# Sixteen tiles transposed by DMA instead of TensorE, and a check and last sums moved earlier in an attention kernel

## The chip, the cores and the metric

The kernel runs on one core of a Trainium2 chip. The metric is the time of one execution on the device in microseconds. Before the change three runs took 743.94, 744.22 and 745.38 us; their median is 744.22 us.

## What is computed

Two blocks on separate inputs of shape (1, 2048, 640), in bf16, 32 heads of 20 columns each; the results stand side by side in an output of (1, 2048, 1280).

```python
# A: softmax attention
scores = jnp.einsum("bhqd,bhkd->bhqk", q, k) * (Dh ** -0.5)
p = _softmax(scores, axis=-1)
o = jnp.einsum("bhqk,bhkd->bhqd", p, v)          # then o @ wo
# B: linear attention
phi = lambda t: jnp.where(t > 0, t + 1, jnp.exp(t)) + 1e-6
kv = jnp.einsum("bhsd,bhse->bhde", pk, v)        # pk = phi(k), pq = phi(q)
num = jnp.einsum("bhqd,bhde->bhqe", pq, kv)
den = jnp.einsum("bhqd,bhd->bhq", pq, z)[..., None] + 1e-6
o = num / den                                     # then o @ wo
```

## The kernel before

The program is one straight list of instructions per engine. Class `_Fast` writes these lists when the kernel is built: `run` steps through a clock of its own, and at each step gives each engine the next operation that its own estimates call ready. The estimates are constants in the code (`_c_dve`, `_c_act`, `_c_pool`, and a number handed to `push` for each operation, `occ` for how long the engine is held and `lat` for when the result is seen). On the chip the lists are fixed and each engine works its list in order; semaphores guard what is read and written. An operation that is late therefore holds up everything behind it on its engine.

**A** is done in 32 rounds `n` (`self.NN`), one for each of 4 query chunks of 512 and 8 groups of 4 heads. A round has 16 key tiles `kt` of 128 keys. TensorE makes the scores of a key tile for four heads into PSUM; then there are two ways to their exponentials. On the common one, ScalarE reads two heads' scores (128x1024) in one ACTIVATE (L1854) and writes `f_PT`; one pass of value matmuls follows. For `DN[n]` of the 16 key tiles of round `n`, VectorE instead makes 16-bit integers from the scores (L1752, four instructions to a key tile, tile `f_Sr`), whose bits, read as bf16, stand for the exponential; GpSimd adds a constant to them twice (L1928), and TensorE takes them through three passes of value matmuls. `DN` sums to 139 of the 512 key tiles of all rounds.

The value matmuls of a round add up in one PSUM bank. `norm` (L1931) then has VectorE transpose that bank into `f_T` (L1958), take the reciprocal of the sums into `f_Rt` (L1949), have the product made (L1951, on GpSimd, in the last round on VectorE) and transposed again into `f_OTn` (L1955). DMAs on SP's queue move the rows to `f_OTd` (L1984), from where the output projection reads them as weights. In the last query chunk that projection comes in two parts: `step_open` makes the sums over all but the last group of heads, 8 of them (4 row tiles, 2 halves), each held in a PSUM bank; `step_close` adds the last group, VectorE (L989) and ScalarE (L988) copy the bank to `f_st`, and SP writes it out (L985).

**The check.** The short way to the exponential holds only for a range of sums. `check` (L2010) has GpSimd compare the reciprocals `f_Rt` with two bounds (L2018, L2020) and VectorE reduce the result (L2022); at the very end `step_flag` folds this to one number, `f_flag`, which all engines load (L2275); were it 0, a general version would run in its place. In the kernel before, the check over rounds 0 to 30 (496 columns) is queued in `normed` when round 30 is finished, and that over round 31 (16 columns) when round 31 is.

**B** is a list of steps (`self.qb`, made by `b_steps`) that TensorE works on where A leaves it time. Each step has a `pace`, the share of A's scores that must be behind it, rising from `B0` to `B1`. For each row tile `t` of the 16: `ndstep` makes numerator and denominator, VectorE divides into `self.o` (L1587, two buffers in `f_ar`); `trstep` transposes the 128x640 result with five TensorE transposes (L1004) into a PSUM bank, and VectorE copies them to `self.oT` (L1610); `ostep` multiplies by B's `wo`, twice 20 matmuls of 32x320, and the result is copied (L989) and written out (L985). `pick_step` picks TensorE's next step from the head of these lists. Before the change it posted a step without matmuls (a load) only when it stood first in `self.qb`.

SP's queue carries nearly all DMAs, in order: the pieces of Q and K that A's later rounds wait for (L1194), the `f_OTd` moves, B's input, which comes from DRAM through DMA transposes of 512x128 (L1362), and the outputs.

Of the kernel before, what the change touches and what calls it, by code (L numbers as in the profile page):

```python
# [7 lines left out]
BF16 = mybir.dt.bfloat16  # L8
# [6 lines left out]
D_MODEL = 640  # L15
# [3 lines left out]
N_DC = 5  # L19
# [749 lines left out]
class _Fast:  # L769
# [10 lines left out]
    WP = 0.7578125  # L780
    FADJ = False
    NX = 1
    DN = (4, 4, 4, 5, 4, 4, 4, 4, 5, 4, 5, 4, 5, 4, 4, 5, 4, 4, 5, 4, 5, 4, 5, 4, 5, 4, 5, 4, 4, 5, 4, 4)
    XD = 2
    HOT = 0
    PVH2 = 11
    B0 = 0.33
    B1 = 0.92
    LASTD = 8
    STEP = 20.0  # L790
    DMIN = -3
# [6 lines left out]
    def __init__(self, nc, sch, es, ps, A_x, A_wqkv, A_wo, B_x, B_wqkv, B_wo, out):  # L798
# [52 lines left out]
        self.pieces = {}  # L851
        self.abank = list(self.AUX)
        self.srr = 0
        self.stq = [[] for _ in range(4)]
        self.sth = {}
        self.log = []
# [534 lines left out]
    def b_steps(self):  # L1391
        ps = self.ps
        sch = self.sch
        NQC = self.NQC
        out = []
# [165 lines left out]
        def ndstep(tc, tl, h):  # L1561
            cs = (0, 1, 2) if h == 0 else (2, 3, 4)
            t = 4 * tc + tl
            key = ("nd", t, h)
            k = t % 2
# [24 lines left out]
            needs = tuple(("bq", tc, c) for c in cs)  # L1590
            p = before(t, 2)
            if p is not None:
                needs += (("tr", p),)
            return _Step(mms, post, needs=needs, key=key)

        def trstep(t):
            k = t % 2
            key = ("tr", t)

            def mms(b):  # L1600
                pb = ps[:, b, :].bitcast(BF16)
                for c in range(N_DC):
                    yield ("F", [dict(tr=True, out=pb[:, 128 * c:128 * (c + 1)], id=self.ident[:],
                                      reads=(("o", k, 0), ("o", k, 1), "ident"), writes=(("ps", b),),
                                      inc=(c == N_DC - 1), **{"in": self.o[:, k, 128 * c:128 * (c + 1)]})], 58.0)

            def post(b):
                pb = ps[:, b, :].bitcast(BF16)
                dst = self.oT[:, k].rearrange("p c m -> p (c m)")
                self.push("dve", lambda e: e.tensor_copy(dst, pb[:, 0:D_MODEL]), (("ps", b),), (("oT", k),),  # L1610
                          400, after=lambda: (self.done.add(key), self.abank.append(b)))
            needs = (("nd", t, 0), ("nd", t, 1))
            p = before(t, 2)
            if p is not None:
                needs += (("bo", p, 0), ("bo", p, 1))
            return _Step(mms, post, needs=needs, key=key)

        def ostep(t, h):
            k = t % 2
            key = ("bo", t, h)  # L1620

            def mms(b):
                for c in range(N_DC):
                    yield ("C", self.quad(b, 0, 320, self.oT[:, k, c, :], self.wB[:, c, D_MODEL + 320 * h:D_MODEL + 320 * (h + 1)],
                                          c == 0, c == N_DC - 1, (("oT", k), ("wB", 1))), 137.0)

            def post(b):
                if ("bs", t) not in self.pieces:
                    self.pieces["bs", t] = self.slot(("b", t))
                self.evac(b, self.pieces["bs", t], ("b", t), h, "dve", 2,  # L1630
                          self.out[128 * t:128 * (t + 1), D_MODEL:2 * D_MODEL], lambda: self.done.add(key))
            return _Step(mms, post, needs=(("tr", t), ("wl", 1, 1)), key=key)

        order_tc = list(range(NQC - 1, -1, -1))
        prev = ("turn", "ld2")
# [325 lines left out]
    def normed(self, n):  # L1961
# [35 lines left out]
                    self.prio.append(self.step_out(t, h, range(5), needs=tuple(  # L1997
                        ("OTs", self.pos[qc, x]) for x in range(N_GRP)), cb=odone))
        if g == N_GRP - 2 and last:
            self.sch.barrier(("dve", "pool"), tuple(x for k in range(self.NQC) for x in self.xt(k)))  # L2000
            for t in range(4 * qc, 4 * qc + 4):
                for h in range(2):
                    self.prio.append(self.step_open(t, h, tuple(("OTs", self.pos[qc, x]) for x in range(6)) + ("expd", "dd")))
            self.check(0, n)
        if g == N_GRP - 1 and last:
            for t in range(4 * qc, 4 * qc + 4):
                for h in range(2):
                    self.prio.append(self.step_close(t, h))
            self.check(n, n)

    def check(self, n0, n1):
        k = 0 if n0 == 0 else 1
# [43 lines left out]
        return self.NN  # L2056

    def pick_step(self, t):
        while self.qb and self.qb[0].mms is None and self.runnable(self.qb[0]):
            st = self.qb.pop(0)  # L2060
            st.post(None)
            self.done.add(st.key)
        for k, st in enumerate(self.prio):
            if st.bank is not None and self.runnable(st):
                gen = st.mms(self.obank[st.bank])
                it = next(gen)
                if self.est("pe", [r for m in it[1] for r in m["reads"]], ()) > t + 30:
                    continue
                self.prio.pop(k)
                return [st, self.obank[st.bank], gen, it]  # L2070
# [11 lines left out]
        for q in cands:  # L2082
# [4 lines left out]
            for k in ks:  # L2087
                st = q[k]
                if st.mms is None:
                    break  # L2090
# [255 lines left out]
```

## Time and profile before

| | |
|---|---|
| median of 3 runs | 744.22 us (743.94 to 745.38) |
| the profiled execution's own time | 744.1 us |
| its span, first to last instruction | 742.3 us |
| instructions | 25718 |
| busy: TensorE, ScalarE, GpSimd, VectorE | 721.4, 711.3, 595.6, 591.1 us |
| ScalarE's ACTIVATE of L1854 | 746, together 698.2 us |
| granted TensorE clock, mean | 0.998 |

The busy time of an engine counts each moment once, also where one instruction starts before the one ahead of it has ended, as ScalarE's and TensorE's do. So the mean of one ACTIVATE (1139 ns) is longer than the step from one to the next. What 1.8 us separate the execution's own time from its span lies outside the instructions.

### The profile page before, as it was taken

The numbers are of one execution on the slowest core, as the hardware profiler recorded it, in microseconds if no ns is written. First come the engines' busy times: TensorE is split into PE (matmuls) and PEld (weight loads), VectorE is DVE, ScalarE is ACT, GpSimd is POOL, SyncE is SP. The second block draws the span as 40 slices with busy tenths as digits, with TensorE's granted clock in tenths as the row PEclk, the third lists the DMA queues.
The fourth block names the chain that finished last, engine by engine and source line by source line (L and its number), as shares of the span: only waits on it lengthen the run. The fifth ranks groups of instructions, "written<-read, shape, count | busy, mean of one in ns | idle before, by whom it ended". The sixth has DMA issues, their size and how long they took to land.

```text
span 742.3 us, 25718 instructions
## 1 busy us (share of the span) xinstructions
PE 721.4 (97%) x11214; PEld 256.0 (34%) x11214; DVE 591.1 (80%) x1136; ACT 711.3 (96%) x806; POOL 595.6 (80%) x359
## 2 busy tenths in 40 slices
PE   8999999999899999999999999999999999999996
PEld 5433333332223333333333333233233333332334
DVE  6888887958747788787879878799898878898962
ACT  4879999999999999999999999999999999999993
POOL 6687798779998787878778779886889778779774
PEclk9999999999999999999999999999999999999999
DMA  8520101007200100201001003011010100000001
GB/s 197 155 48 16 32 14 35 13 21 149 45 10 18 39 9 15 37 6 41 17 11 33 23 7 95 13 42 36 17 42 33 32 30 16 12 31 15 15 28 42
DMA packets 42610, 27.67 MB, mean 37 GB/s; under 512 B 26890, under 2 KB 41930, under 8 KB 42490
## 3 DMA queue, kind: packets, MB, share of 16 engines
q1 hardware_dynamic: 41178, 25.62, 13.5%
q8 instruction: 90, 1.47, 0.8%
q10 hardware_dynamic: 1312, 0.33, 0.2%
q14 instruction: 30, 0.25, 0.1%
HBM read 8.40 MB, written 5.24 MB: 18 GB/s over the span
## 4 chain that ended last, share of the span: by engine, by line
ACT 69%; PE 21%; POOL 4%; DVE 2%; DMA 1%; SPq 1%; issue 0%; ACTq 0%; DVEq 0%
ACT f_PT L1854 67%; PE ps L155 21%; ACT ps L1385 3%; POOL f_Sr L1928 3%; DMA f_ar<-in_A_wqkv_dram 1%; DVE f_Sr L1752 1%; SPq L1194 1%; DMA f_KT<-f_ar 0%; DVE f_ar L1234 0%; POOL f_ar L1419 0%; POOL f_ar L1416 0%; DVE f_KT L1255 0%; POOL f_xT L2020 0%; POOL f_xT L2018 0%; POOL f_ar L1422 0%
## 5 line engine op out<-in xcount | busy, mean ns | idle before, releaser
L1854 ACT ACTIVATE f_PT<-ps 128x1024 bf16<-128x1024 f32 x746 | 698.2, 1139 | 15.2 <-PE ps L155 14.5
L1928 POOL TENSOR_SCALAR f_Sr<-f_Sr 128x2048 int16<-128x2048 int16 x278 | 527.4, 1897 | 87.5 <-PE ps L155 67.1
L1752 DVE TENSOR_SCALAR f_Sr<-ps 128x512 int16<-128x512 f32 x556 | 376.0, 684 | 73.4 <-PE ps L155 65.8
L155 PE MATMUL ps<-f_Qr,f_KT 32*128 32x512 bf16 x2048 | 293.4, 384 | 7.3 <-ACT f_PT L1854 5.0
L155 PEld LDWEIGHTS ps<-f_Qr,f_KT 32*128 32x128 bf16 x2048 | 74.0, 91 | 250.1 <-ACT f_PT L1854 233.4
L155 PE MATMUL ps<-f_ar 128*32 128x320 bf16 (+4 forms) x3024 | 152.1, 295 | 1.5 <-DVE f_Sr L1752 0.7
L155 PE MATMUL ps<-f_PT,f_V 128*21 128x512 bf16 x1492 | 141.7, 383 | 0.0
L155 PE MATMUL ps<-f_Sr,f_V 128*21 128x512 bf16 x1112 | 100.9, 382 | 2.1 <-POOL f_Sr L1928 1.9
L155 PEld LDWEIGHTS ps<-f_ar 128*32 128x32 bf16 x3024 | 61.1, 95 | 65.3 <-issue 35.2
L1951 POOL TENSOR_TENSOR f_T<-f_T,f_Rt 128x512 bf16<-128x512 f32 x31 | 32.5, 1048 | 41.5 <-DVE f_Rt L1949 40.0
L155 PE MATMUL ps<-f_Sr,f_Vp 128*21 128x512 bf16 x556 | 54.8, 382 | 0.2 <-POOL f_Sr L1928 0.2
L155 PEld LDWEIGHTS ps<-f_PT,f_V 128*21 128x21 bf16 x1492 | 35.7, 90 | 47.0 <-issue 40.9
L1387 DVE SCALAR_TENSOR_TENSOR f_ar<-ps,f_ar 128x320 bf16<-128x320 f32 (+1 forms) x52 | 29.2, 561 | 13.7 <-ACT ps L1385 13.0
L155 PE MATMUL ps<-f_ar,f_xT 128*32 128x160 bf16 x1280 | 37.1, 234 | 1.3 <-DMA f_ar<-in_A_wqkv_dram 0.7
L155 PEld LDWEIGHTS ps<-f_Sr,f_V 128*21 128x21 bf16 x1112 | 25.4, 90 | 34.1 <-issue 23.0
L989 DVE CAST f_st<-ps 128x320 bf16<-128x320 f32 x60 | 28.5, 479 | 10.1 <-PE ps L155 10.1
L1383 DVE TENSOR_SCALAR f_ar<-ps 128x320 f32<-128x320 f32 (+1 forms) x52 | 29.0, 558 | 7.7 <-PE ps L155 7.5
L1385 ACT ACTIVATE ps<-ps 128x320 f32<-128x320 f32 (+1 forms) x52 | 33.4, 643 | 0.0
L155 PE MATMUL ps<-f_wo,f_OTd 128*32 128x320 bf16 (+1 forms) x608 | 32.7, 302 | 0.0
L155 PE MATMUL ps<-f_xT,f_ar 128*32 128x512 bf16 x400 | 30.3, 383 | 0.3 <-DVE f_xT L1168 0.2
L155 PEld LDWEIGHTS ps<-f_ar,f_xT 128*32 128x32 bf16 x1280 | 24.0, 96 | 17.6 <-issue 8.9
L155 PE MATMUL ps<-f_xT,f_wq 128*32 128x512 bf16 x320 | 25.2, 383 | 0.0
(76 smaller groups left out, 325.1 us busy)
## 6 DMA issues: line engine op xcount, KB each, us to landing
out_dram<-f_st SPq DMA_DIRECT2D x32, 160.0 KB
f_ar<-in_B_wqkv_dram SPq DMA_DIRECT2D x3, 800.0 KB
f_OTd<-f_OTn SPq DMA_DIRECT2D x105, 20.0 KB
f_Qr<-f_sq SPq DMA_DIRECT2D x88, 20.0 KB
f_KT<-f_ar SPq DMA_DIRECT2D x22, 80.0 KB
f_ar<-in_A_wqkv_dram SPq DMA_DIRECT2D x2, 800.0 KB
f_wq<-in_A_wqkv_dram SPq DMA_DIRECT2D x1, 800.0 KB
f_wo<-in_A_wo_dram SPq DMA_DIRECT2D x1, 800.0 KB
```

Source lines behind the costliest of these rows:

```text
L155: lambda e: e.matmul(out, lhsT, rhs, start=start, stop=stop, tile_position=tp, skip_group_check=sgc),
L989: (lambda e: e.tensor_copy(sl, ps[:, b, 0:320])), (("ps", b),), (("stage", s, h),),
L1194: self.push("sp", lambda e, d=d, a=a, m=m: e.dma_start(d, src[a:a + m, :]), rs, res, 710, prio=n if which == "Q" else g, after=after, ok=okd)
L1383: self.push("dve", lambda e: e.tensor_scalar(r1, src, 0.0, 1e-6, op0=ALU.max, op1=ALU.add), (("ps", b),), (rk,), _c_dve(n), prio=1, ok=ok, ...
L1385: "act", lambda e: e.activation(src, src, AF.Exp), (), (("ps", b),), _c_act(n), prio=0,
L1387: "dve", lambda e: e.scalar_tensor_tensor(dst, src, 1.0, r1, op0=ALU.min, op1=ALU.add),
L1752: post = lambda: self.push("dve", lambda e: e.tensor_scalar(self.Sr[:, s, i, :], self.ps[:, b, :], 0.0, 32639.0 - self.PH[-1], op0=ALU.max ...
L1854: return _Op("act", lambda e: e.activation(self.PT[:, s0:s0 + n, :], ps[:, b0:b0 + n, :], AF.Exp, scale=math.log(2.0) / 128.0, bias=self.l ...
L1928: return e.tensor_scalar(v, v, inc, 1.0, op0=ALU.add, op1=ALU.mult)
L1951: nmul, lambda e: e.tensor_tensor(T2v, Tv, R.unsqueeze(2).broadcast_to([128, 16, 32]), op=ALU.mult),
```

## The change

The change has four parts.

1. `trstep` has no matmuls any more. Its `issue` puts five DMA transposes of 128x128 on SP's queue, from `self.o` to `self.oT`, both in on-chip memory (L1603 of the changed kernel); the code gives each 1300 ns of SP's time and 3500 ns to its landing. `ostep` waits for each of the five pieces by itself. 80 TensorE transposes and 16 VectorE copies go, 80 DMA transposes come.
2. `check` over the first rounds is queued as soon as the last Q is made and A has no preparing steps left; it then covers the rounds that are finished (0 to 27, 448 columns), and the last check covers rounds 28 to 31 (64 columns).
3. Three of the eight `step_open` no longer wait for the last ACTIVATE (`expd`) but for the last VectorE key tile (`dd`) and for B's list to be empty (`bfin`).
4. `DN` is 1 smaller in rounds 27 and 29, so it sums to 137, and `B1` is 0.93. `pick_step` posts a load or a transposing step wherever it stands in the first eight of B's list.

```diff
-    DN = (..., 5, 4, 4, 5, 4, 4)
+    DN = (..., 5, 3, 4, 4, 4, 4)
-    B1 = 0.92
+    B1 = 0.93
...
-            def mms(b):
-                pb = ps[:, b, :].bitcast(BF16)
+            def issue(b):
                 for c in range(N_DC):
-                    yield ("F", [dict(tr=True, out=pb[:, 128 * c:128 * (c + 1)], id=self.ident[:],
...
-                self.push("dve", lambda e: e.tensor_copy(dst, pb[:, 0:D_MODEL]), (("ps", b),), (("oT", k),),
-                          400, after=lambda: (self.done.add(key), self.abank.append(b)))
+                    self.push("sp", lambda e, c=c: e.dma_start_transpose(
+                        self.oT[:, k, c, :], self.o[:, k, 128 * c:128 * (c + 1)]),
+                        (("o", k, 0), ("o", k, 1)), (("oT", k, c),), 1300, prio=40, lat=3500,
+                        after=(lambda: self.done.add(("trd", t))) if c == N_DC - 1 else None)
...
         if g == N_GRP - 2 and last:
-            self.sch.barrier(("dve", "pool"), tuple(x for k in range(self.NQC) for x in self.xt(k)))
             for t in range(4 * qc, 4 * qc + 4):
                 for h in range(2):
-                    self.prio.append(self.step_open(t, h, tuple(("OTs", self.pos[qc, x]) for x in range(6)) + ("expd", "dd")))
-            self.check(0, n)
+                    self.prio.append(self.step_open(t, h, tuple(("OTs", self.pos[qc, x]) for x in range(6)) + (
+                        ("dd", "bfin") if 2 * (t % 4) + h < 3 else ("expd", "dd"))))
...
+        if last and self.chk < 0 and ("Q", self.NN - 1) in self.done and not self.qa:
+            self.sch.barrier(("dve", "pool"), tuple(x for k in range(self.NQC) for x in self.xt(k)))
+            self.chk = n
+            self.check(0, n)
...
-        while self.qb and self.qb[0].mms is None and self.runnable(self.qb[0]):
-            st = self.qb.pop(0)
+        for st in [x for x in self.qb[:8] if x.mms is None and self.runnable(x)]:
+            self.qb.remove(st)
```

What this does to the lists shows at three places. The first is VectorE's list at its end. Before, the reduction of the check (L2022) stands ahead of the last round's transpose (L1958):

```order
L989 CAST f_st<-ps 128x320 x2
L2022 TENSOR_REDUCE f_gm<-f_xT 128x1
L1958 STREAM_TRANSPOSE f_T<-ps 128x512
L1949 RECIPROCAL f_Rt<-f_T 128x16
L1951 TENSOR_TENSOR f_T<-f_T,f_Rt 128x512
L1955 STREAM_TRANSPOSE f_OTn<-f_T 128x512
```

The same place in the changed list (its line numbers differ a little: L1953 is L1958 of before, L1944, L1946 and L1950 are L1949, L1951 and L1955, L2021 is L2022):

```order
L990 CAST f_st<-ps 128x320 x2
L1953 STREAM_TRANSPOSE f_T<-ps 128x512
L1944 RECIPROCAL f_Rt<-f_T 128x16
L1946 TENSOR_TENSOR f_T<-f_T,f_Rt 128x512
L1950 STREAM_TRANSPOSE f_OTn<-f_T 128x512
L2021 TENSOR_REDUCE f_gm<-f_xT 128x1
```

The first reduction has left this place; the one of the last check stands behind the norm, as before.

The second is GpSimd's list where the first check now stands, three norms (L1946) from the end:

```order
L1923 TENSOR_SCALAR f_Sr<-f_Sr 128x2048 x7
L2017 TENSOR_SCALAR f_xT<-f_Rt 128x448
L2019 TENSOR_SCALAR f_xT<-f_Rt 128x448
L1946 TENSOR_TENSOR f_T<-f_T,f_Rt 128x512
L1923 TENSOR_SCALAR f_Sr<-f_Sr 128x2048 x9
```

and VectorE's list beside it:

```order
L1953 STREAM_TRANSPOSE f_T<-ps 128x512
L1388 SCALAR_TENSOR_TENSOR f_ar<-ps,f_ar 128x512
L1944 RECIPROCAL f_Rt<-f_T 128x16
L990 CAST f_st<-ps 128x320
L2021 TENSOR_REDUCE f_gm<-f_xT 128x1
L1747 TENSOR_SCALAR f_Sr<-ps 128x512 x2
L1950 STREAM_TRANSPOSE f_OTn<-f_T 128x512
```

The two comparisons and the reduction now stand between the work of a running round, ahead of GpSimd's product and of two of VectorE's score conversions.

The third is SP's list where B's first result tiles (L1603) come in, between B's input, the `f_OTd` moves and the pieces of Q:

```order
L1363 DMA_TRANSPOSE f_ar<-in_B_x_dram 128x512 x3
L1603 DMA_TRANSPOSE f_ar<-f_ar 128x128 x9
L1979 DMA f_OTd<-f_OTn 20x512 x3
L1979 DMA f_OTd<-f_OTn 4x512
L1979 DMA f_OTd<-f_OTn 16x512
L1603 DMA_TRANSPOSE f_ar<-f_ar 128x128 x5
L1195 DMA f_Qr<-f_sq 12x512
```

Before, the five loads of L1362 stood there in one piece, and the moves and the pieces of Q followed without anything between them.

## Rows read from the trace of the kernel before

**Rows 1.** The page's first part: busy time, share of the span and instructions.

```profile
PE 721.4 (97%) x11214; PEld 256.0 (34%) x11214; DVE 591.1 (80%) x1136; ACT 711.3 (96%) x806; POOL 595.6 (80%) x359
```

**Rows 2.** Busy time of each engine by stretch, granted clock, DMA share.

```profile
core 0: us, PE busy (x) PEld busy (x) DVE busy (x) ACT busy (x) POOL busy (x), PEclk, DMA share, GB/s
226.00:300.00 74.00, 73.01 (x1146) 25.63 (x1146) 58.88 (x108) 73.92 (x86) 61.59 (x35) 1.00 0.08 24
300.00:400.00 100.00, 99.69 (x1590) 34.85 (x1594) 81.22 (x151) 100.00 (x120) 77.61 (x43) 1.00 0.10 22
...
600.00:690.00 90.00, 88.12 (x1249) 28.55 (x1250) 75.03 (x145) 89.95 (x104) 72.85 (x41) 1.00 0.06 19
690.00:710.00 20.00, 19.64 (x325) 7.70 (x317) 18.42 (x47) 19.98 (x23) 15.76 (x9) 1.00 0.06 21
710.00:729.00 19.00, 18.22 (x257) 6.50 (x259) 7.25 (x14) 18.99 (x21) 17.49 (x10) 1.00 0.06 21
```

**Rows 3.** The chain that ended last, by time: start us, us, what.

```profile
546.56 69.72 ACT f_PT L1854 x76
...
629.11 46.76 ACT f_PT L1854 x51
```

**Rows 4.** Timeline of the end: start us, us, engine, line, operation, [idle before <-releaser].

```profile
714.13 14.86 ACT L1854 ACTIVATE f_PT<-ps 128x1024 bf16<-128x1024 f32 x16
...
715.72 22.47 SPq L985 DMA_DIRECT2D out_dram<-f_st  x6
...
729.34 0.48 PE L155 MATMUL ps<-f_PT,f_V 128*21 128x512 bf16 x4
...
729.56 0.82 PE L155 MATMUL ps<-f_wo,f_OTd 128*32 128x320 bf16 x16
...
730.24 0.82 PE L155 MATMUL ps<-f_wo,f_OTd 128*32 128x320 bf16 x16
...
730.76 1.19 DVE L2022 TENSOR_REDUCE f_gm<-f_xT 128x1 f32<-128x992 f32 x1 [9.29 <-POOL f_xT L2020]
...
731.86 0.71 DVE L1958 STREAM_TRANSPOSE f_T<-ps 128x512 f32<-128x512 f32 x1
...
734.39 1.13 PE L155 MATMUL ps<-f_wo,f_OTn 128*32 128x320 bf16 x28 [1.12 <-DVE f_OTn L1955]
734.83 1.68 DVE L989 CAST f_st<-ps 128x320 bf16<-128x320 f32 x4 [0.43 <-PE ps L155]
...
736.45 0.42 ACT L988 CAST f_st<-ps 128x320 bf16<-128x320 f32 x1 [0.41 <-PE ps L155]
736.62 0.14 DVE L2036 TENSOR_SCALAR f_flag<-f_g 1x1 int32<-1x1 f32 x1
```

**Rows 5.** Groups of instructions by line: busy us, mean ns, idle before, releasers.

```profile
L1928 POOL TENSOR_SCALAR f_Sr<-f_Sr 128x2048 int16<-128x2048 int16 x278 | 527.4, 1897 | 87.5 <-PE ps L155 67.1
L1752 DVE TENSOR_SCALAR f_Sr<-ps 128x512 int16<-128x512 f32 x556 | 376.0, 684 | 73.4 <-PE ps L155 65.8 <-DMA f_KT<-f_ar 0.7
L1004 PE MATMUL ps<-f_id,f_ar 128*128 128x128 bf16 x100 | 10.1, 222 | 0.0
L1610 DVE COPY f_ar<-ps 128x640 bf16<-128x640 bf16 x16 | 7.4, 475 | 0.1
```

**Rows 6.** GpSimd's check and its wait ahead of the norm's product, from the timeline.

```profile
710.79 1.05 POOL L1951 TENSOR_TENSOR f_T<-f_T,f_Rt 128x512 bf16<-128x512 f32 x1 [3.44 <-DVE f_Rt L1949]
...
727.73 1.45 POOL L2018 TENSOR_SCALAR f_xT<-f_Rt 128x496 f32<-128x496 f32 x1
...
729.27 1.46 POOL L2020 TENSOR_SCALAR f_xT<-f_Rt 128x496 f32<-128x496 f32 x1
```

**Rows 7.** SP's DMAs by line: duration of the issue, ns min/median/max.

```profile
L1362 SPq DMA_TRANSPOSE f_ar<-in_B_x_dram x30: 1156/1258/1949, 171.3 to 551.5; - x30
...
L985 SPq DMA_DIRECT2D out_dram<-f_st x32: 332/338/1338, 235.6 to 737.8; - x32
```

**Rows 8.** Two landings after their issue, from the chain that ended last.

```profile
2.25 7.64 DMA f_ar<-in_A_wqkv_dram
...
167.77 2.39 DMA f_KT<-f_ar
```

More of the change, by code (lines that the diff above doesn't have):

```diff
@@ L782 @@
     NX = 1
-    DN = (4, 4, 4, 5, 4, 4, 4, 4, 5, 4, 5, 4, 5, 4, 4, 5, 4, 4, 5, 4, 5, 4, 5, 4, 5, 4, 5, 4, 4, 5, 4, 4)
+    DN = (4, 4, 4, 5, 4, 4, 4, 4, 5, 4, 5, 4, 5, 4, 4, 5, 4, 4, 5, 4, 5, 4, 5, 4, 5, 4, 5, 3, 4, 4, 4, 4)
     XD = 2
@@ L853, in __init__ @@
         self.srr = 0
+        self.chk = -1
         self.stq = [[] for _ in range(4)]
@@ L1592, in ndstep @@
             if p is not None:
-                needs += (("tr", p),)
+                needs += (("trd", p),)
             return _Step(mms, post, needs=needs, key=key)
@@ L1598, in trstep @@
             key = ("tr", t)
-            def mms(b):
-                pb = ps[:, b, :].bitcast(BF16)
+            def issue(b):
                 for c in range(N_DC):
-                    yield ("F", [dict(tr=True, out=pb[:, 128 * c:128 * (c + 1)], id=self.ident[:],
[L1604 to L1609, printed above, removed]
-                self.push("dve", lambda e: e.tensor_copy(dst, pb[:, 0:D_MODEL]), (("ps", b),), (("oT", k),),
-                          400, after=lambda: (self.done.add(key), self.abank.append(b)))
+                    self.push("sp", lambda e, c=c: e.dma_start_transpose(
+                        self.oT[:, k, c, :], self.o[:, k, 128 * c:128 * (c + 1)]),
+                        (("o", k, 0), ("o", k, 1)), (("oT", k, c),), 1300, prio=40, lat=3500,
+                        after=(lambda: self.done.add(("trd", t))) if c == N_DC - 1 else None)
             needs = (("nd", t, 0), ("nd", t, 1))
@@ L1615, in trstep @@
                 needs += (("bo", p, 0), ("bo", p, 1))
-            return _Step(mms, post, needs=needs, key=key)
+            return _Step(None, issue, needs=needs, key=key)
         def ostep(t, h):
@@ L1624, in mms @@
                     yield ("C", self.quad(b, 0, 320, self.oT[:, k, c, :], self.wB[:, c, D_MODEL + 320 * h:D_MODEL + 320 * (h + 1)],
-                                          c == 0, c == N_DC - 1, (("oT", k), ("wB", 1))), 137.0)
+                                          c == 0, c == N_DC - 1, (("oT", k, c), ("wB", 1))), 137.0)
             def post(b):
@@ L1631, in post @@
                           self.out[128 * t:128 * (t + 1), D_MODEL:2 * D_MODEL], lambda: self.done.add(key))
-            return _Step(mms, post, needs=(("tr", t), ("wl", 1, 1)), key=key)
+            return _Step(mms, post, needs=(("trd", t), ("wl", 1, 1)), key=key)
         order_tc = list(range(NQC - 1, -1, -1))
@@ L2008, in normed @@
                     self.prio.append(self.step_close(t, h))
-            self.check(n, n)
+            assert self.chk >= 0
+            self.check(self.chk + 1, n)
+        if last and self.chk < 0 and ("Q", self.NN - 1) in self.done and not self.qa:
+            self.sch.barrier(("dve", "pool"), tuple(x for k in range(self.NQC) for x in self.xt(k)))
+            self.chk = n
+            self.check(0, n)
     def check(self, n0, n1):
@@ L2058, in pick_step @@
     def pick_step(self, t):
-        while self.qb and self.qb[0].mms is None and self.runnable(self.qb[0]):
-            st = self.qb.pop(0)
+        for st in [x for x in self.qb[:8] if x.mms is None and self.runnable(x)]:
+            self.qb.remove(st)
             st.post(None)
             self.done.add(st.key)
+        if not self.qb and not self.qa:
+            self.done.add("bfin")
         for k, st in enumerate(self.prio):
@@ L2089, in pick_step @@
                 if st.mms is None:
-                    break
+                    continue
                 if self.runnable(st) and st.bank is None:
```

## The prediction

> **What bounds the kernel now.** I read the busy shares first, then the same by stretch, then the chain of waits, then the end instruction by instruction. By busy shares TensorE is at 97% and ScalarE at 96% [rows 1], so either could be the bound. By stretch ScalarE has no idle time to speak of from 226 to 729 us: 73.92 of 74, 100.00 of 100, 89.95 of 90, 19.98 of 20, 18.99 of 19 us [rows 2], while TensorE's share moves with what it is given. The chain of waits says how fast ScalarE goes: 76 ACTIVATEs in 69.72 us are 0.917 us each, 51 in 46.76 us are 0.917 us again [rows 3]. The pace is the same in stretches where TensorE had much beside the scores and where it had little, so it is ScalarE's own. Hence: from about 226 us on, ScalarE's last ACTIVATE ends when its work is done, at 714.13 + 14.86 = 728.99 us [rows 4], and only two things move the end: how much work ScalarE gets, and how long the tail behind its last ACTIVATE is. That tail is 742.3 - 729.0 = 13.3 us now.
>
> In the tail the reader is to see one wait. The last value matmuls start at 729.34 us and take 0.48 us, so the bank is complete at 729.82; but VectorE starts the transpose L1958 at 731.86 only, because the check's reduction L2022 stands ahead of it on VectorE and itself waited for GpSimd's two comparisons (idle 9.29 us ahead of it, end about 731.9) [rows 4]. From L1958 it is 2.53 us to the closing matmuls (734.39), 0.44 us more to the first copy (734.83), and the last copy ends at 736.45 + 0.42 = 736.87 [rows 4]. The output DMAs and the loading of the flag fill the rest to 742.3.
>
> **The change part by part.**
>
> *DN from 139 to 137.* Two key tiles go from VectorE and GpSimd to ScalarE. A key tile is four heads' scores, an ACTIVATE takes two, so ScalarE gets 2 x 2 = 4 ACTIVATEs more. At 0.917 us [rows 3] that is **+3.67 us** on an engine without gaps. What it takes away is 8 conversions of 684 ns on VectorE (5.5 us) and 4 additions of 1897 ns on GpSimd (7.6 us) [rows 5]; both engines have idle time (GpSimd is busy 72.85 of 90 us from 600 to 690 [rows 2]), so that is worth nothing by itself.
>
> *TensorE's transposes.* Of the 100 of L1004, 20 belong to the start (A's own input); 80 go, 80% of 10.1 us, 8.1 us, and 16 copies, 7.4 us, on VectorE [rows 5]. They lie beside ScalarE's work, which did not wait for them: ScalarE's idle time in all the stretches shown is 0.16 us. I cost their removal at **0**; at most it returns that 0.16 us.
>
> *80 DMA transposes on SP.* No row shows one from on-chip memory to on-chip memory. The nearest are the 30 from DRAM, of four times the size: 1.16 us to issue at least, 1.26 us in the middle, 1.95 us at most [rows 7]. 80 of them are some 100 us of SP's time, spread over more than 200 us. Between issue and landing the rows have 2.39 us for a move within the chip and 7.64 us for an 800 KB load at the start [rows 8]. The lists were written for 1.3 us of issue and 3.5 us from the issue's start to landing. I take 1.26 us and a landing about 2.4 us later, 3.7 us from the start, by the row that is nearest in kind, which about meets what the list allows; so TensorE comes to `oT` when it is there, and I take **0**. Below nothing it can't be worth anything, since ScalarE does not wait for B's tiles. The other bound is the rival below. The queue behind matters too: pieces of Q and `f_OTd` moves now stand behind DMAs that wait for VectorE's division. The next round's Q is moved about a round ahead, so I see no price in it.
>
> The trace has a TensorE transpose at 222 ns [rows 5] and SP's time for a DMA transpose at 1258 ns [rows 7]. The Trainium skill, "VectorE: DVE Perf Modes", section "The three transpose paths", gives 390 ns on TensorE against 1309 ns by DMA for 128x128 in bf16, and its rules for kernel authors say to use TensorE where a PSUM destination will do, which speaks against this change. By its figures 80 x (1309 - 390) = 73.5 us would be added, by the rows 80 x (1258 - 222) = 82.9 us; both are sums over two queues that ScalarE does not wait for, so the term in my sum is 0 by either.
>
> *The check moved forward.* In the tail L2022 is no longer ahead of the transpose. TensorE's last value matmuls still stand behind two of the opening sums, at 730.24 - 729.56 = 0.68 us each [rows 4]; these can start when the last but one ACTIVATE has freed its banks, 0.92 us before ScalarE's end, and finish 0.45 us behind it. So the last value matmuls start some 0.4 us behind ScalarE's end as they do now (729.34 - 728.99 = 0.35), and the transpose follows at about +1.0 us instead of +2.87 (731.86 - 728.99): **-1.9 us**. The reduction of 64 columns instead of 16 still ends ahead of the first copy.
>
> Where it now stands, GpSimd needs about 448/496 of 1.45 + 1.46 us [rows 6], 2.6 us, where the code plans 2 x (0.93 x 448 + 75) = 983 ns. So it comes 1.6 us late by the list. What hides this: GpSimd waited 3.44 us for the reciprocal ahead of the norm's product in the round before the last [rows 6], and the comparisons stand just ahead of such a product. Behind the reduction on VectorE wait two score conversions, whose banks TensorE wants. If the gap covers all, the price is 0; if VectorE waits the full 1.6 us and TensorE with it, ScalarE, which has one group of scores in hand (0.92 us), loses some 0.7 to 1.6 us. I take **+0.2 us**, near the covered end, because of that gap.
>
> *The last sums.* Now 7 openings are done before the closings, and the eighth (0.68 us) stands behind them, so the last copy waits 0.41 us on ScalarE [rows 4]. With three openings made early all eight are ready. ScalarE's four copies then end with VectorE's, near 736.5 instead of 736.87. SP's last output follows; one of its issues took up to 1338 ns where 338 is usual [rows 7]. But the flag, ready at 736.62 + 0.14 us [rows 4], stands behind VectorE's four copies as before. I take **-0.3 us**, between 0 and 0.9 us.
>
> *Sum*, against the profiled execution: 744.1 + 3.67 - 1.9 + 0.2 - 0.3 = 745.8 us. That execution is 0.1 us under the median of 744.22, so I leave it. It is 1.6 us above the median, 0.21%.
>
> **The rivals.**
>
> *A: the forecast*, between 745.0 (tail -0.9 and no wait for the check) and 747.0 (the check costs 1.4 us).
>
> *B: the two sides cancel.* The tail gives all it can (-1.9 - 0.9), the check hides fully, and the 0.16 us come back: 744.1 + 3.67 - 2.8 - 0.16 = 744.8 us, from 744.3 to 745.3. For it: SP's long issue sits in the tail, and GpSimd's gap is long enough. Against it: the flag's own path is not shortened after the copies.
>
> *C: faster.* ScalarE's pace is really TensorE's: ACTIVATEs overlap, a busy row says little of what an engine waits for, and TensorE is at 99.69 of 100 us from 300 to 400 [rows 2]. Then the 8.1 us of transposes taken from TensorE come back in the place where B's second half runs. A third of them (2.7 us) gives 745.8 - 2.7 = 743.1 us, which is still no change; from 3.1 us on, 38% of them, it is faster, and all of them give 737.7 us. It decides if the step between ACTIVATEs falls under 0.917 us in the second half. Against it: 0.917 us in both long runs [rows 3], and 18.99 of 19 us for ScalarE in a stretch where TensorE had only 18.22 [rows 2]. That the change is made as written shows in the lists, so a rival in which it does nothing is left out but for this one.
>
> *D: the DMA transposes land late.* Landing at 5 us and more from the issue, TensorE, which works in order, stands at the matmuls of `oT`, with the scores behind them. Sixteen tiles; ScalarE has one group in hand, so each tile costs what goes beyond about 0.9 us. At 0.5 us for half of the tiles it is 745.8 + 4 = 749.8 us, at 0.5 us for all 753.8. For it: the DMA from DRAM took up to 7.64 us [rows 8] and SP's queue is in order. Against it: B's steps are paced and small.
>
> **How the numbers follow.** A measurement of this kernel can tell about 0.2% from no change, so "same" is 742.7 to 745.7 us. Chances: A 0.50, B 0.27, C 0.06, D 0.17. A's band lies half above 745.7 and half below. Faster by over 0.2%: half of C and a little for what I don't see, 0.05. Slower: D and a little more than half of A, 0.17 + 0.29 = 0.46, and I round it to 0.48 for a wait that I have not named. Same: 0.47. The predicted time is A's 745.8. The range of 8 in 10 takes in A and B and the mild end of D: 744.4 to 748.2 us. A's own range is 745.0 to 747.0 us.
>
> **What would show it.** Right: 750 ACTIVATEs at 0.917 us; ScalarE's last end near 732.7 us; the transpose of the last round about 1 us behind it; eight closings in one piece; tail about 11.1 us instead of 13.3; no new idle time on ScalarE from 226 us on. Wrong, towards B or C: ScalarE's last end clearly under 732 us, which can only be if the pace is not its own. Wrong, towards D: TensorE or ScalarE idle in the second half, released by a DMA into `f_ar`; towards the upper end of A: VectorE's L2021 with an idle time before it, released by GpSimd, and ScalarE's idle time right after.

## The result, and the profile after

The changed kernel takes **747.89 us** (median of 20 runs, 746.59 to 755.06), the kernel before, run beside it, 744.64 us. The ratio is 1.0038 with a 95% interval of 1.0020 to 1.0056: slower by 0.2% to 0.6%. Forecast were 745.8 us, and a range of 744.4 to 748.2 us. The profiled execution took 748.07 us, its span is 746.2 us.

Read again in the order of the prediction. First what ScalarE has to do and what it waited for, from the pages of the two kernels (line, engine, operation, tiles, count | busy time, mean ns | idle time before and its releaser); L1849 is L1854 of before. Before:

```profile
L1854 ACT ACTIVATE f_PT<-ps 128x1024 bf16<-128x1024 f32 x746 | 698.2, 1139 | 15.2 <-PE ps L155 14.5
L155 PE MATMUL ps<-f_ar 128*32 128x320 bf16 (+4 forms) x3024 | 152.1, 295 | 1.5 <-DVE f_Sr L1752 0.7
```

In the changed kernel:

```profile
L1849 ACT ACTIVATE f_PT<-ps 128x1024 bf16<-128x1024 f32 x750 | 701.8, 1117 | 16.2 <-PE ps L155 15.5
L155 PE MATMUL ps<-f_ar 128*32 128x320 bf16 (+4 forms) x3024 | 152.9, 295 | 3.0 <-DMA f_ar<-f_ar 1.7
```

There are 750 ACTIVATEs instead of 746, as DN has it, with 1.0 us more idle time before them. New is the releaser in the second row: TensorE stood 1.7 us at B's matmuls until a DMA from `f_ar` to `f_ar` had landed, which are B's transposes. Where ScalarE lost time stands in the stretches (the columns of [rows 2]: length, busy time of PE, PEld, DVE, ACT and POOL, granted clock, DMA share, GB/s), first one of before, then two of the changed kernel:

```profile
500.00:600.00 100.00, 99.08 (x1472) 32.73 (x1464) 88.97 (x170) 100.00 (x113) 79.77 (x45) 1.00 0.11 32
```
```profile
500.00:600.00 100.00, 98.32 (x1455) 31.96 (x1451) 86.18 (x164) 99.64 (x111) 81.66 (x45) 1.00 0.18 46
...
710.00:729.00 19.00, 17.77 (x260) 5.69 (x256) 6.14 (x12) 18.32 (x20) 13.00 (x8) 1.00 0.16 48
```

ScalarE was gapless there before (100.00 of 100 us in the first stretch, 18.99 of 19 us in the second [rows 2]); now it lacks 0.36 us of 100 and 0.68 us of 19. The chain of waits of the changed kernel shows the second place (start, length, what):

```profile
709.56 0.63 SPq L1603
710.23 2.33 DMA f_ar<-f_ar
712.61 1.00 PE ps L155 x11
713.61 0.41 SPq L1603
714.07 1.23 SPq L1603
715.34 3.13 DMA f_ar<-f_ar
718.51 0.66 PE ps L155 x6
719.20 14.81 ACT f_PT L1849 x16
```

SP issues the transposes of B's last tiles one behind the other, as a rule 1.23 us each. The two landings in this chain come 2.3 and 3.1 us after their issue has ended; TensorE waits for them, and ScalarE behind it. SP itself has no pause there (its timeline):

```profile
686.62 13.34 SPq L1603 DMA_TRANSPOSE f_ar<-f_ar  x9
700.00 3.06 SPq L1979 DMA_DIRECT2D f_OTd<-f_OTn  x4
703.11 15.11 SPq L1603 DMA_TRANSPOSE f_ar<-f_ar  x11
```

For 31.6 us the 24 DMAs stand end to end. Four of these 20 transposes took 1.56 to 2.63 us to issue, together 2.9 us more than the 1.3 us that the list gives to each, and nothing in the queue takes that up. In the first stretch TensorE waited for no transpose; what happened there shows in the comparison with plain copies below. The end of the changed kernel, instruction by instruction (idle time before and its releaser in brackets):

```profile
719.20 15.72 ACT L1849 ACTIVATE f_PT<-ps 128x1024 bf16<-128x1024 f32 x17 [0.27 <-PE ps L155]
735.87 0.72 DVE L1953 STREAM_TRANSPOSE f_T<-ps 128x512 f32<-128x512 f32 x1 [13.95 <-PE ps L155]
738.33 0.28 DVE L2021 TENSOR_REDUCE f_gm<-f_xT 128x1 f32<-128x128 f32 x1
738.41 1.27 PE L155 MATMUL ps<-f_wo,f_OTn 128*32 128x320 bf16 x32 [0.53 <-DVE f_OTn L1950]
```

ScalarE's last ACTIVATE ends at 719.20 + 15.72 = 734.92 us, 5.93 us later than before [rows 4]. The transpose starts 0.95 us behind it and waits for TensorE alone; the eight closings run in one piece; the tail is 746.2 - 734.92 = 11.3 us instead of 13.3.

Of the 5.93 us some 0.7 are from the loading at the start, in which executions differ. The row of ScalarE that begins behind the last long wait of the start stands at 203.70 us in the kernel before and at 204.38 us in the changed one (their timelines, ScalarE):

```profile
203.70 23.21 ACT L1854 ACTIVATE f_PT<-ps 128x1024 bf16<-128x1024 f32 x25 [0.98 <-PE ps L155]
```
```profile
204.38 22.30 ACT L1849 ACTIVATE f_PT<-ps 128x1024 bf16<-128x1024 f32 x24 [0.98 <-PE ps L155]
```

In the run below in which TensorE is relieved of transposes the lists up to there are those of before, and the same row begins at 204.60 us.

So 5.25 us are to be explained; four ACTIVATEs are 3.67 of them, and 1.6 us are left. ScalarE waits for TensorE five times from 500 to 735 us, 1.04 us of idle time in all. Counted from the start of one ACTIVATE to the start of the next, these waits cost the 1.6 us, since an ACTIVATE that has to wait no longer overlaps the one ahead of it. The theory that went into the experiments: 3.67 us for DN, 1.6 us because DMA transposes land too late, 2 us back in the tail.

### The profile page after: what moved, and what is told of

Read it like the earlier page. It is cut to its first block, busy times and chain, and to the rows that moved or that the text cites. A ratio compares the mean times of both kernels' runs of the same rounds, so it can differ in the third digit from the quotient of the medians.

```text
span 746.2 us, 25617 instructions
## 1 busy us (share of the span) xinstructions
PE 721.7 (97%) x11142; PEld 252.7 (34%) x11142; DVE 580.9 (78%) x1112; ACT 715.5 (96%) x810; POOL 588.0 (79%) x355
## 4 chain that ended last, share of the span: by engine, by line
ACT 63%; PE 26%; DVE 3%; POOL 3%; DMA 1%; SPq 1%; issue 1%; ACTq 0%; DVEq 0%
ACT f_PT L1849 61%; PE ps L155 26%; ACT ps L1386 3%; POOL f_Sr L1923 2%; DMA f_ar<-f_ar 1%; DVE f_Sr L1747 1%; SPq L1195 1%; SPq L1979 0%; DMA f_KT<-f_ar 0%; SPq L1603 0%; DVE f_KT L1256 0%; POOL f_ar L1498 0%; PE ps L1093 0%; DVE f_T L1953 0%; DVE f_sq L1219 0%
## 5 line engine op out<-in xcount | busy, mean ns | idle before, releaser
L1849 ACT ACTIVATE f_PT<-ps 128x1024 bf16<-128x1024 f32 x750 | 701.8, 1117 | 16.2 <-PE ps L155 15.5
L1923 POOL TENSOR_SCALAR f_Sr<-f_Sr 128x2048 int16<-128x2048 int16 x274 | 519.8, 1897 | 112.8 <-PE ps L155 90.8
L1747 DVE TENSOR_SCALAR f_Sr<-ps 128x512 int16<-128x512 f32 x548 | 370.2, 684 | 81.1 <-PE ps L155 74.2
L155 PE MATMUL ps<-f_PT,f_V 128*21 128x512 bf16 x1500 | 144.1, 383 | 0.0
L155 PE MATMUL ps<-f_Sr,f_V 128*21 128x512 bf16 x1096 | 99.0, 382 | 2.1 <-POOL f_Sr L1923 1.8
L155 PEld LDWEIGHTS ps<-f_ar 128*32 128x32 bf16 x3024 | 62.7, 95 | 65.8 <-issue 36.5
L1946 POOL TENSOR_TENSOR f_T<-f_T,f_Rt 128x512 bf16<-128x512 f32 x31 | 32.5, 1048 | 26.0 <-DVE f_Rt L1944 24.2
L1953 DVE STREAM_TRANSPOSE f_T<-ps 128x512 f32<-128x512 f32 x32 | 22.6, 707 | 14.4 <-PE ps L155 14.4
```

The lines of the kernel that those rows point to most:

```text
L155: lambda e: e.matmul(out, lhsT, rhs, start=start, stop=stop, tile_position=tp, skip_group_check=sgc),
L1747: post = lambda: self.push("dve", lambda e: e.tensor_scalar(self.Sr[:, s, i, :], self.ps[:, b, :], 0.0, 32639.0 - self.PH[-1], op0=ALU.max ...
L1849: return _Op("act", lambda e: e.activation(self.PT[:, s0:s0 + n, :], ps[:, b0:b0 + n, :], AF.Exp, scale=math.log(2.0) / 128.0, bias=self.l ...
L1923: return e.tensor_scalar(v, v, inc, 1.0, op0=ALU.add, op1=ALU.mult)
L1946: nmul, lambda e: e.tensor_tensor(T2v, Tv, R.unsqueeze(2).broadcast_to([128, 16, 32]), op=ALU.mult),
L1953: self.push("dve", lambda e: e.transpose(self.T[:], ps[:, b, :]), (("ps", b),), ("T",), 630, prio=-1, after=freed, ok=lambda: n == 0 or (" ...
```

## The experiments

### Plain copies in the place of the transposes

```diff
-                    self.push("sp", lambda e, c=c: e.dma_start_transpose(
-                        self.oT[:, k, c, :], self.o[:, k, 128 * c:128 * (c + 1)]),
+                    self.push("sp", lambda e, c=c: e.dma_start(
+                        out=self.oT[:, k, c, :], in_=self.o[:, k, 128 * c:128 * (c + 1)]),
```

> The changed kernel with its 80 DMA transposes issued as plain DMAs of the same 128x128 pieces, so that B's half is not the reference's; every engine's list and all planned times stay. Theory (the 1.6 us of new ScalarE idle time come from the DMA transposes being late, because SP needs about 1.23 us to issue each one): a plain DMA within the chip issues in about 0.34 us, so the gaps of ScalarE at 711 to 719 us go and the time falls by 1.0 to 1.6 us, to 746.3 to 746.9. Rival (the gaps belong to the new order of the lists or to DN): the gaps stay, 747.9 within 0.4.

746.03 us, ratio to before 1.0010 (0.9987 to 1.0032): 1.9 us under the changed kernel by medians, a little more than the 1.0 to 1.6 us expected. L1603 as the trace groups it (count: min/median/max ns, first and last start; below it who waited), in the changed kernel and with plain copies:

```profile
L1603 SPq DMA_TRANSPOSE f_ar<-f_ar x80: 1096/1230/2632, 484.4 to 716.7; - x80
...
who waited for it (us, times):
  PEld ps L155: 3.5, 6
  DVE f_ar L1588: 3.5, 2
  PE ps L155: 1.7, 5
```
```profile
L1603 SPq DMA_DIRECT2D f_ar<-f_ar x80: 465/593/1463, 484.9 to 709.5; - x80
```

Nobody waited for the plain ones. They take half the issue time (0.59 us; the 0.34 us expected is the row of the outputs [rows 7]), and the last starts 7.2 us earlier. In the changed kernel two engines waited: TensorE, for the pieces of `oT`, and VectorE (L1588, B's division), which may not write a buffer of `o` before the transposes have read it. ScalarE with plain copies (timeline):

```profile
204.88 21.22 ACT L1849 ACTIVATE f_PT<-ps 128x1024 bf16<-128x1024 f32 x23 [1.02 <-PE ps L155]
...
725.21 8.54 ACT L1849 ACTIVATE f_PT<-ps 128x1024 bf16<-128x1024 f32 x9
```

It ends at 733.75 us, 4.76 later than before, of which 1.18 stand at the start already. The 3.58 us between are the four ACTIVATEs (3.67). So the two terms are told apart: DN costs what it was costed at, the DMA transposes 1.6 to 1.9 us.

Both kernels have the same lists, so ScalarE's ACTIVATEs can be set side by side one by one. The changed kernel begins 0.50 us ahead (204.38 against 204.88 us), is level at 586.51 us and 1.3 us behind at 719.20 us. The 1.3 us come from 711 us on, with TensorE's waits for transposes. The 0.5 us ahead of that come another way: the transposes hold up other DMAs behind them on SP. A copy of VectorE waits 0.96 us for an output to leave `f_st`, and the conversions behind it, TensorE and ScalarE come later. The same copy in the changed kernel and with plain copies:

```profile
581.03 0.49 DVE L990 CAST f_st<-ps 128x320 bf16<-128x320 f32 x1 [0.96 <-DMA out_dram<-f_st]
```
```profile
580.39 0.43 DVE L990 CAST f_st<-ps 128x320 bf16<-128x320 f32 x1
```

### Four ACTIVATEs cut short

```diff
+        def exp(e, m=512):
+            return e.activation(
+                self.PT[:, s0:s0 + n, 0:m], ps[:, b0:b0 + n, 0:m], AF.Exp, scale=math.log(2.0) / 128.0,
+                bias=self.lng - 127.0 * math.log(2.0))
-        return _Op("act", lambda e: e.activation(
...
+        return _Op("act", (lambda e: exp(e, 8)) if j in (640, 655, 685, 700) else exp,
```

> The changed kernel with four of its 750 ACTIVATEs, two each around rounds 27 and 29 or 30, cut from 1024 columns to 16 (the exponentials of the rest are left out); lists unchanged. Theory (ScalarE sets the end, 0.917 us for each): if a short one still costs a fifth, the time falls by 2.9 us, at most by 3.67: 744.2 to 745.0. Rival (TensorE sets the pace, and four ACTIVATEs more or less are hidden): ScalarE has idle time instead and the time stays at 747.9 within 0.4.

748.51 us, ratio 1.0065 (1.0035 to 1.0096): no fall at all. ScalarE's rows from 600 to 710 us say why; one of the four places in its timeline:

```profile
645.02 7.45 ACT L1850 ACTIVATE f_PT<-ps 128x1024 bf16<-128x1024 f32 x8 [0.42 <-PE ps L155]
```

Behind each short ACTIVATE the next one waits for its scores, 2.1 us in four waits out of at most 3.67 gained. `SB` holds two pairs of score banks: the next scores are made in the pair that the ACTIVATE before has just freed, so they are not there earlier because this one is short. Another 0.7 us went ahead of the first of the four, where ScalarE has 98.97 us of work from 500 to 600 us instead of 99.64.

The experiment did not measure what it was meant to. Idle time on ScalarE and no gain is what its rival expected, so by itself it does not speak against TensorE's pace; the next two runs do. It shows that time taken off an ACTIVATE is not had back while the next scores come no earlier. What four ACTIVATEs cost is shown by the run above.

### Sixteen small ACTIVATEs more

```diff
+            if e == "act" and op.seq in self.again:
+                b0 = self.again[op.seq]
+                self.sch.op(e, lambda h: h.activation(
+                    self.spare[:], self.ps[:, b0, 0:192], AF.Exp, scale=math.log(2.0) / 128.0,
+                    bias=self.lng - 127.0 * math.log(2.0)), (("ps", b0),), ("spare",))
```

> The kernel before with 16 more ACTIVATEs of 128x192 on ScalarE, each just ahead of one of the ordinary ones between the 632nd and the 722nd, reading the same scores into a spare tile; all lists otherwise unchanged. From the 128x1024 step of 0.917 us and the 128x320 step of 0.33 us one of 192 columns is some 0.22 us, 16 are 3.6 us. Theory (ScalarE is the bound in this direction: what is added is paid in full, though what is taken away is not, since TensorE is only 0.2 us behind it): 748.2, from 747.6 to 748.8. Rival (TensorE sets the pace and ScalarE has as much room as it): 744.6 to 745.6.

750.02 us beside 744.26, ratio 1.0067 (1.0041 to 1.0093). Paid in full, and above the expected range, since each costs more than was estimated: in ScalarE's timeline the next ACTIVATE starts 641.87 - 641.51 = 0.36 us behind the start of a small one, at another place 0.42 us, not 0.22. The 16 of them are 6.5 us together, beside 5.8 us between the medians.

```profile
641.51 0.33 ACT L962 ACTIVATE f_dup<-ps 128x192 bf16<-128x192 f32 x1
641.87 5.61 ACT L1863 ACTIVATE f_PT<-ps 128x1024 bf16<-128x1024 f32 x6
```

Had TensorE set the pace, it would have hidden them.

### TensorE relieved of B's transposes

```diff
+            if m.get("tr") and m["reads"][0][0] == "o" and not m["inc"]:
+                continue
             if m.get("tr"):
...
-                self.push("dve", lambda e: e.tensor_copy(dst, pb[:, 0:D_MODEL]), (("ps", b),), (("oT", k),),
+                self.push("dve", lambda e: e.tensor_copy(dst, pb[:, 0:128].unsqueeze(1).broadcast_to([128, N_DC, 128])), (("ps", b),), (("oT", k),),
```

VectorE copies the one piece that is left five times.

> The kernel before with one of the five TensorE transposes of each of B's tiles instead of five (64 of 80 left out, so B's half is not the reference's); lists otherwise unchanged. TensorE loses 64 x 0.1 us = 6.5 us of work. Theory (ScalarE does not wait for them): 744.6 within 0.3. Rival C (the pace is TensorE's): 38% to all of it comes back, 742.2 to 738.1.

744.83 us, ratio 0.9994 (0.9970 to 1.0018), as expected. TensorE's rows of these transposes fall from 10.1 us for 100 [rows 5] to 5.0 us for 36; the 6.5 us were an estimate. The 5.1 us taken from TensorE come back nowhere. Rival C is out from this side too.

### The early check and the early sums alone

```diff
-            self.check(0, n)
...
+                        ("dd", "bfin") if 2 * (t % 4) + h < 3 else ("expd", "dd"))))
...
+        if last and self.chk < 0 and ("Q", self.NN - 1) in self.done and not self.qa:
+            self.chk = n
+            self.check(0, n)
```

> The kernel before with the early check and the three early last sums of the changed kernel, and nothing else of it: TensorE transposes, DN of 139, B1 of 0.92. Theory (the early check takes 1.9 us off the tail, the sums 0.3, the DMA transposes and DN are what costs): 742.4, from 742.0 to 743.0, faster than both kernels. Rival (what the tail gives is lost where the check now stands, on GpSimd): 744.6 within 0.4, with idle time on VectorE ahead of the early reduction and on ScalarE behind it.

742.96 us beside 744.64, ratio 0.9981 (0.9964 to 0.9997): faster than both kernels. ScalarE ends at 727.50 + 3.11 = 730.61, so the tail is 740.9 - 730.61 = 10.3 us, 3.0 less than before. But the forecast's +0.2 for the check's new place is 1.2 us here, so the time is in the expected range by two errors that cancel (timeline from 660 to 670 us of GpSimd, VectorE and ScalarE):

```profile
661.62 1.33 POOL L2023 TENSOR_SCALAR f_xT<-f_Rt 128x448 f32<-128x448 f32 x1
663.03 1.34 POOL L2025 TENSOR_SCALAR f_xT<-f_Rt 128x448 f32<-128x448 f32 x1
664.40 1.09 DVE L2027 TENSOR_REDUCE f_gm<-f_xT 128x1 f32<-128x896 f32 x1 [1.22 <-POOL f_xT L2025]
667.36 2.86 ACT L1855 ACTIVATE f_PT<-ps 128x1024 bf16<-128x1024 f32 x3 [1.19 <-PE ps L155]
```

Two comparisons take 2.7 us where the list has 0.98; VectorE waits 1.22 us for the second, TensorE 1.13 us for the transpose that stands behind the reduction on VectorE, ScalarE 1.19 us for its scores. In the changed kernel the same two stand at 662.89 and 664.30 us, and the reduction, at 668.19, waits for nothing. It is the same mechanism, covered there and not here.

### The same with the comparisons' true cost in the list

```diff
-                  _c_pool(w), prio=3, after=lambda: self.push(
+                  (1420 if w > 64 else _c_pool(w)), prio=3, after=lambda: self.push(
```

(The second comparison likewise.)

> The kernel before with the early check and the early sums, and the list told what GpSimd's two early comparisons cost on the chip (1420 ns each instead of 492), so that VectorE's reduction is put further back. Theory (the 1.19 us of ScalarE idle time at 667 us in the run without this were VectorE waiting for the second comparison): that gap goes, the tail stays at 10.3 us, 741.8, from 741.3 to 742.3. Rival (the gap moves to another wait or the new order costs as much): 743.0 within 0.4.

**741.79 us** beside 744.26, ratio 0.9951 (0.9928 to 0.9974). That is the fastest kernel of this study, 2.5 us under the kernel before and 6.1 under the changed one by medians: TensorE's transposes, DN of 139, early check, early sums, and a list that knows what GpSimd needs. The reduction, now at 668.17 us, waits for nothing, and ScalarE has no gap there; the tail is 740.9 - 730.14 = 10.7 us. With the sums as before and all else alike:

```diff
-                        ("dd", "bfin") if 2 * (t % 4) + h < 3 else ("expd", "dd"))))
+                        ("expd", "dd"))))
```

> The kernel before with the early check alone, its comparisons at 1420 ns in the list; the last sums as before. It splits the tail's gain. By the prediction's terms (1.9 us for the check, 0.3 for the sums) it is 742.7, 0.3 us over the run with the sums. Rival (the sums give as much as 1.1 us, since 3.0 us came off the tail where 2.2 were expected): the transpose still starts 1 us behind ScalarE, but the closings or the last copies come later, and the time is 0.8 to 1.1 us over the run with the sums.

742.42 us, ratio 0.9975 (0.9944 to 1.0006). The early sums are worth 0.6 us by medians, between the two expectations; the intervals overlap too far to say more.

### TensorE's transposes back in the changed kernel

`trstep` as in the kernel before, in the changed one:

```diff
-            return _Step(None, issue, needs=needs, key=key)
+            return _Step(mms, post, needs=needs, key=key)
```

> The changed kernel with B's transposes back on TensorE (and VectorE's 16 copies), DN of 137 and all else as in the change. Theory (the DMA transposes cost the 1.5 us by which the run with plain copies was earlier, and give nothing back): 746.4, up to 747.1 if the new order of the lists costs something. Rival (with DN of 137 TensorE needs the 8.1 us that the DMA transposes take from it): 748 or more, with ScalarE idle in the second half and TensorE full.

746.83 us, ratio 1.0027 (1.0001 to 1.0053), within what was expected: 1.1 us under the changed kernel by medians, though the intervals of the two ratios overlap. The list is made anew, and it has a wait of its own. The chain from 570 to 585 us is TensorE's own work, and ScalarE goes on behind it at 581.85 us, after 1.09 us without work:

```profile
573.49 8.34 PE ps L155 x131
...
581.85 3.77 ACT f_PT L1855 x4
```

This kernel and the one with the early check and sums alone (742.96 us) differ in DN, B1 and the order in which loads are posted, and in nothing else; on ScalarE each has one wait of its own, of 1.09 and 1.19 us. The 3.9 us between their medians are the nearest that two runs come to DN alone, without any DMA transpose.

### DMA transposes with DN as before

Two kernels have DMA transposes, early check and sums, but DN and B1 of before. They were to show that the four ACTIVATEs and the lateness can both be had back.

```diff
-    DN = (..., 5, 3, 4, 4, 4, 4)
+    DN = (..., 5, 4, 4, 5, 4, 4)
-    B1 = 0.93
+    B1 = 0.92
-                        (("o", k, 0), ("o", k, 1)), (("oT", k, c),), 1300, prio=40, lat=3500,
+                        (("o", k, 0), ("o", k, 1)), (("oT", k, c),), 1250, prio=40, lat=3500,
```

> The changed kernel with DN of 139 and B1 of 0.92 as before, and 1250 instead of 1300 ns of SP's time for each DMA transpose in the list (its landing still at 3500 ns). ScalarE gets 746 ACTIVATEs again. Theory (four ACTIVATEs of DN cost 3.67 us, late DMA transposes 1.5): 744.2, from 743.6 to 745.0, with waits on DMA transposes as before. Rival (the DMA transposes need what DN gives up; the lists with 139 are slower by as much): 746 to 748.

753.80 us, ratio 1.0101 (1.0069 to 1.0134). The theory falls here, and the time is above what the rival allowed too. The second kernel:

> The same with a landing of 4500 ns in the list instead of 3500, and 1420 ns for each of GpSimd's early comparisons. Theory (the DMA transposes cost only by being later than the list says): nobody waits for them, ScalarE ends near 729.5 us and the time is 742.3, from 741.6 to 743.0, within 0.5 us of the same lists' kind with TensorE transposes (741.8). Rival (they cost something whatever the list knows: SP's time, the outputs and pieces of Q behind them): 743.5 to 745, with other transfers late.

749.02 us, ratio 1.0047 (1.0018 to 1.0077), again above theory and rival. TensorE's matmuls still waited 4.7 us for transposes and VectorE 6.1 us, so a landing that is too short in the list is not all of it. Rows of L1603 in the first of the two, and a piece of its chain of waits:

```profile
L1603 SPq DMA_TRANSPOSE f_ar<-f_ar x80: 1096/1231/2514, 485.9 to 729.9; - x80
...
  DVE f_ar L1588: 9.6, 3
  PEld ps L155: 8.3, 6
  PE ps L155: 6.3, 4
```
```profile
521.03 0.62 SPq L1195
521.70 1.12 SPq L1603
522.86 1.23 SPq L1603
524.14 1.23 SPq L1603
525.41 4.20 DMA f_ar<-f_ar
529.66 0.67 PE ps L155 x7
530.35 7.44 ACT f_PT L1849 x8
```

The transposes queue on SP behind moves of `f_OTd` and pieces of Q, follow each other at 1.16 to 1.28 us from start to start, and the last one here lands 4.20 us after its issue has ended. In the second kernel a wait for one is followed by a second loss (stretches of 5 us, columns as in [rows 2]: PE is the first busy time, the granted clock the third number from the end):

```profile
525.00:530.00 5.00, 2.85 (x37) 0.64 (x34) 1.98 (x3) 3.10 (x4) 4.76 (x4) 0.79 0.12 24
530.00:535.00 5.00, 5.00 (x50) 1.55 (x51) 2.47 (x4) 3.08 (x4) 3.10 (x2) 0.53 0.43 137
```

TensorE works 2.85 us of 5 while it waits for the transposes. Then the granted clock is at its lower level, 1.2 GHz (0.50 of full speed in each us from 528 to 534), and in the second stretch TensorE is full while ScalarE still has only 3.08 us of work. No stretch of the changed kernel up to 729 us shows that; its waits are shorter.

Is it the transposes, or these lists? The same lists with plain copies:

> The kernel with DMA transposes, DN of 139 and a landing of 3500 ns in the list (the run of 753.8 us), with the 80 DMA transposes issued as plain DMAs of the same pieces, so that B's half is not the reference's; every list unchanged. Theory (the waits of TensorE and VectorE on DMA transposes are the whole of the 9 us, and ScalarE has 746 ACTIVATEs): 744.2, from 743.5 to 745.2, nobody waiting for the plain DMAs. Rival (lists with DN of 139 and the transposes on SP stall for other reasons, SP's queue among them): 747 or more.

744.73 us, ratio 1.0000 (0.9982 to 1.0018), and nobody waits for L1603. So all of the 9.1 us between the medians 753.80 and 744.73 come from issuing these DMAs as transposes, the lower clock behind the waits included. (The executions of the slower kernel spread from 749.54 to 758.94 us, so the 9.1 us are rough.) The lists have waits of their own besides, in both: ScalarE has 2.1 us of idle time with plain copies too, and VectorE's early reduction waits 0.85 us for the second comparison. What of the 9.1 us is SP's time and what the landing was not tried apart.

## Why the prediction was right, and where it was not

The time fell into the range, but only into the part added for the mild end of rival D: A's own range ends at 747.0 us. It fell on the side held most likely, slower by more than 0.2%, and that was close to a toss-up (0.48 against 0.47). It came out 2.1 us above the forecast (2.3 us by the profiled execution, 0.7 of them from the start, which no term was about). Step by step, against the profiled execution:

- **DN, +3.67 us**: right. 3.58 us in the run in which no transpose is late, 3.9 us between the medians of two kernels with TensorE's transposes.
- **TensorE's transposes, 0**: right. Leaving 64 of 80 out changes the time by a factor of 0.9994.
- **80 DMA transposes, 0**: the step that failed; 1.6 us by ScalarE's rows, 1.9 us by medians. The numbers for one transpose were near (1.23 us of issue against 1.26, landings 2.3 and 3.1 us later against 2.4). Two conclusions were not. "So TensorE comes to `oT` when it is there": the prediction took one transpose at a time, with SP's time "spread over more than 200 us" (and its own 3.7 us were already more than the 3.5 us of the list). On the chip SP issued 20 transposes and 4 moves without a pause from 686.62 to 718.22 us, four issues took 1.56 to 2.63 us, and TensorE stood waiting at `oT`; that is 1.3 us of it. And "so I see no price in it", for the DMAs that stand behind the transposes: an output came late, and VectorE waited for it; that is where the other 0.5 us begin. In kind this is rival D, whose sign (TensorE idle in the second half, released by a DMA into `f_ar`) came true, at 1.6 us instead of its 4 to 8.
- **The tail, -1.9 and -0.3 us**: 2.0 us together, right within 0.2. With lists of their own it is 2.1 (check alone: 741.0 - 729.80) to 3.0 us.
- **The check's new place, +0.2 us**: 0 in the changed kernel, 1.2 in another list. The bound 0 to 1.6 held; in these runs it went by the place.

The sum with the measured terms, and 0.7 us from the start: 744.1 + 3.67 + 1.6 - 2.0 + 0.7 = 748.07 us, which is what the execution took. It closes by itself, since the 1.6 us were what was left over; what stands for them independently is the run with plain copies.

What the prediction did not see is that what the transposes cost hangs on the lists around them. DN and the transposes were costed apart, 3.67 and 0. With DN and B1 as before (and 1250 ns for an issue) the same transposes cost 9.1 us, with the changed kernel's numbers 1.6 to 1.9. The smaller DN may be what lets the transposes be mostly hidden; whether DN, B1 or the order that they happen to give does it was not told apart. Nor does the smaller DN cost 3.67 us in every list: with plain copies on SP the kernels with 137 and 139 take 746.03 and 744.73 us, only 1.3 us apart, as the lists with 139 have waits of their own.

Rival C (TensorE's pace) is refuted by two runs (sixteen ACTIVATEs more, 64 transposes less). Rival B had nothing lost on the transposes and 2.8 us off the tail; the runs show 1.6 us lost and 2.0 us off. The Trainium skill, "VectorE: DVE Perf Modes", section "Rules for kernel authors", has TensorE for a 128x128 transpose where a PSUM destination will do. By medians these runs agree: with all else of the change 746.83 us against 747.89, and with DN and B1 as before, the early check and sums and the measured cost of the comparisons 741.79 us against 749.02. It is not the sum over the queue that decided (80 x 1.23 = 98 us of SP's time made the kernel less than 2 us longer) but where the queue was full, and who waited at its end.

## What to carry over

An operation moved to a queue with time to spare is free only if its result is ready when an engine that works in order comes to it, and if nothing that waits behind it in the queue is wanted sooner. Cost the whole batch where it stands closest, with what is ahead of it in that queue and its longest issue, not one operation with its median and the queue with its average. Where a list is made from planned durations, first put in the measured ones: an error of 0.85 us in each of two GpSimd operations was worth 1.2 us of the kernel's time. And a change that bundles a retuned constant with a new operation is best split with the lists held fixed, by exchanging the operation in its place.

## What the runs showed of the hardware that was not expected

- A DMA transpose of 128x128 within the chip holds SP 1.23 us, a plain DMA of the same piece 0.59 us (medians of 80), and both now and then more than twice as long (2.63 and 1.46 us). The longest landing in the chains shown is 4.20 us after the issue.
- A short ACTIVATE of 128x192 costs 0.36 to 0.42 us from start to start (15 of 16), where the line through 128x1024 and 128x320 gives 0.22.
- In the kernel of 749.02 us a wait of TensorE of 1.81 us was followed by some 6 us at the lower clock level (granted 0.50), with a row of four matmuls of 512 columns at 0.64 us where 0.40 is usual. Not every such wait was: in the kernel of 753.80 us TensorE waited 1.74 us up to 518.02 us, and the granted clock stayed at 1.00. The rows of the first:

```profile
528.61 0.46 PE L155 MATMUL ps<-f_ar 128*32 128x320 bf16 x4 [1.81 <-DMA f_ar<-f_ar]
528.85 0.64 PE L155 MATMUL ps<-f_PT,f_V 128*21 128x512 bf16 x4
```
